# Products of 64 weight rows on the two row halves of the array, in a gated layer that goes by pairs of feature tiles

## The chip, the cores and the metric

The kernel runs on one core of a Trainium2 chip. The metric is the device time of one execution in microseconds (us). The kernel before takes 2023.67 us, the median of three runs that lie between 2023.3 and 2027.02.

## The reference

Four layers act in turn on x, 2048 tokens by 448 features: attention, gated layer, attention, gated layer. Both pairs use the same weights. Cut to what matters here:

```
def _B_ref(x, w_gate, w_up, w_down):      # x: 1 x 2048 x 448, F = 1792
    g = x @ w_gate                        # 448 x 1792
    u = x @ w_up                          # 448 x 1792
    return (sigmoid(g) * u) @ w_down      # 1792 x 448

x = x + _A_ref(layernorm(x), wqkv, wo)    # attention, 16 heads of 28
x = x + _B_ref(layernorm(x), w_gate, w_up, w_down)
x = x + _A_ref(layernorm(x), wqkv, wo)
x = x + _B_ref(layernorm(x), w_gate, w_up, w_down)
```

All inputs are float32.

## The kernel before

**Numbers in two halves.** TensorE multiplies 16-bit floats. A float32 operand is therefore split into a high float16 and a low float16 that holds the rest (`split`, line 170: the high part by ScalarE, the rest by VectorE). A product of two such operands is three products: high x high, high weights x low activations, low weights x high activations.

**The contraction of 448.** 448 rows are three tiles of 128 and a tail of 64. For the tail the high and the low part of the activations share one tile: `split_tail` (line 175) puts the high part on partitions 0 to 63 and the low part on 64 to 127. The weight tiles hold the last 64 rows twice, on both halves (`load_rows`, line 163). One product of the high weights with that tail tile thus gives two terms, and one of the low weights gives the last one (and the product of both low parts, which is too small to matter). So `by_features` (line 350) makes 3 x 3 + 2 = 11 matrix products of 128 x 128 weights with 512 tokens, all added up in one PSUM bank.

**The gated layer.** `gated` (line 977) goes over 4 blocks of 512 tokens and in each over 14 tiles of 128 hidden features. For a tile it makes the 11 products of the gate (bank 4), asks ScalarE for the sigmoid, makes the 11 products of up (bank 5), and asks VectorE for the product of both (line 1033) and `split` for its two halves `hhl`. The down products (`down`, line 991: 12 products of 448 columns, added up in banks 0 to 3 over all 14 tiles) run one tile later, behind the gate and up products of the next tile, so that the pointwise work has time. When a block's 14 tiles are added up, VectorE adds the result to x.

**The other work in the layer.** The next block of tokens is made ready along the way. `steps` (line 293) gives seven steps, taken one per feature tile from the third tile on by `run_fill`: `norm` (statistics on VectorE, the power on GpSimd), `squares` (scaling and 32 x 32 transposes on VectorE), `store` and `gather` (four DMAs to DRAM, two from the SyncE queue and two from ScalarE's, and two back, from SyncE), two empty steps, and two of `ready`, which split the 128-row tiles 0 and 1, then 2 and the tail. In the last block of the first layer `before_next` asks for the next layer's weights at feature tile 6. The first block of a layer is made ready in the output projection of the attention (`out_project`, line 922).

**What sets the order.** The program order is written by hand; nothing reorders it. Each engine takes its instructions in order and waits where a semaphore says so. SBUF is given out in slots from two lists, `big` (19 slots) and `qrt` (12), first freed first used. A name in the profile such as `sig_q` or `xhl_s` is the tile's name and its list.

**Array shapes.** The scores and the mix of attention (lines 821 and 839) use four strips of 32 columns of the array, by `tile_position`. The norm products of the projection (lines 485 and 488) have 16 weight columns and so use one strip. All others, apart from a few small ones at the start, use the full array.

Of the kernel before, what the change touches and what calls it, by code (L numbers as in the profile page):

```python
# [13 lines left out]
F16 = mybir.dt.float16  # L14
I32 = mybir.dt.int32
AF = mybir.ActivationFunctionType
ALU = mybir.AluOpType
AX = mybir.AxisListType

P = 128  # L20
# [6 lines left out]
NB = 4  # L27
TB = NT // NB
W = TB * P
NF = F // P  # L30
# [7 lines left out]
PS = 2.0 ** -14  # L38
# [45 lines left out]
def interleaved_layers(ctx: ExitStack, tc: tile.TileContext, x_in, wqkv, wo, w_gate, w_up,  # L84
                       w_down, out):
    nc = tc.nc
# [6 lines left out]
    big = Slots(spool, "s", N_SLOTS)  # L93
    qrt = Slots(spool, "q", N_QUART)
# [4 lines left out]
    def new_banks():  # L99

        if banks["stack"] is not None:
            banks["stack"].close()
        uid[0] += 1
        banks["stack"] = ExitStack()
        banks["pool"] = banks["stack"].enter_context(
            tc.tile_pool(name=f"psum{uid[0]}", bufs=1, space=bass.MemoryType.PSUM,
                         reuse_waits="tile"))

    def psum(tag, name, shape):
        uid[0] += 1  # L110
        return banks["pool"].tile(shape, F32, name=f"{name}_{uid[0]}", tag=tag, bufs=1)
# [4 lines left out]
    def bank(i, name):  # L116
        return psum(f"bank{i}", name, [P, 512])


    x = cpool.tile([P, NT, D], F32, name="x")  # L120
# [11 lines left out]
    up = cpool.tile([P, 7], F32, name="up")  # L132
# [37 lines left out]
    def split(hi, lo, raw):  # L170

        nc.scalar.copy(hi, raw)  # L172
        nc.vector.tensor_tensor(lo, raw, hi, op=ALU.subtract)  # L173

    def split_tail(tail, raw):

        nc.scalar.copy(tail[0:64], raw[0:64])
        nc.vector.tensor_tensor(tail[64:128], raw[0:64], tail[0:64], op=ALU.subtract)  # L178
# [38 lines left out]
    class Block:  # L217


        def __init__(self, b):  # L220
            self.b = b

        def norm(self, js=range(TB)):
            b = self.b
# [17 lines left out]
                                    op0=ALU.subtract, op1=ALU.mult)  # L242

        def parts(self):
            self.all = big.get("xhl", [P, 7, W], F16)
            self.hi, self.lo = self.all[:, 0:3, :], self.all[:, 3:6, :]
            self.tail = self.all[:, 6, :]


        def squares(self, js=range(TB)):  # L250
# [30 lines left out]
        def part(self, kt):  # L281

            raw = self.raw[:, kt, :].rearrange("p (i t c) -> p t i c", i=4, t=TB)
            order = "p (t i c) -> p t i c"
            if kt < 3:
                hi = self.hi[:, kt, :].rearrange(order, t=TB, i=4)
                lo = self.lo[:, kt, :].rearrange(order, t=TB, i=4)
                split(hi, lo, raw)
            else:
                split_tail(self.tail.rearrange(order, t=TB, i=4), raw)  # L290
                big.put(self.raw)

        def steps(self):
# [56 lines left out]
    def by_features(pm, blk, wh, wl, first_tile=None):  # L350

        order = [(wh, blk.hi), (wh, blk.lo), (wl, blk.hi)]
        terms = [(w(kt), x[:, kt, :]) for kt in range(3) for w, x in order]
        tails = [(w(3), blk.tail) for w in (wh, wl)]
        if first_tile == 0:
            terms = terms[0::3] + terms[2::3] + terms[1::3] + tails
        elif first_tile == 1:
            terms = terms[0::3] + terms[1::3] + tails[0:1] + terms[2::3] + tails[1:2]
        else:
            terms += tails  # L360
        for i, (w, x) in enumerate(terms):
            nc.tensor.matmul(pm, w, x, start=(i == 0), stop=(i == len(terms) - 1))  # L362

    def by_tokens(pm, hi, lo, tail, w, kts=range(4)):

# [93 lines left out]
    gate_scale = nc.scalar.alloc_register("gate_scale")  # L459

    def run_fill(fill, n=1):
        for _ in range(n):
            if fill:
                fill.popleft()()
# [457 lines left out]
    def out_project(outs, gate):  # L922
        new_banks()
        nc.scalar.activation(warm, warm, AF.Sigmoid)
        nc.scalar.reg_load(gate_scale, back.bitcast(I32)[0:1, 3:4])
        first = Block(0)
        steps = first.steps()
        steps = deque(steps[:5] + [lambda: None] * 4 + steps[5:])
        early = 6

        def products(pm, t, kts):
            by_tokens(pm, outs.hi(t), outs.lo(t), outs.tail(t) if 3 in kts else None, gate.out,
                      kts)

        def add(pm, t):
            nc.vector.scalar_tensor_tensor(x[:, t, :], pm, back[:, 1:2], x[:, t, :],  # L936
                                           op0=ALU.mult, op1=ALU.add)

        gate.load_dn()
        gate.load_gu()  # L940
        pms = [bank(t, "op")[:, 0:D] for t in range(early)]
        for t in range(early):
            products(pms[t], t, range(3))
        for t in range(early):
            products(pms[t], t, [3])
            add(pms[t], t)
            if t >= TB - 1:
                run_fill(steps)
        for t in range(early, NT):
            pm = bank(t % 6, "op")[:, 0:D]  # L950
            products(pm, t, range(4))
            add(pm, t)
            run_fill(steps)
        big.put(*outs.kt, gate.out)
        run_fill(steps, 9)
        return first
# [20 lines left out]
    def gated(layer, first, wt, before_next):  # L977
        last = layer == LAYERS - 1
        gu, dn = wt.gu, wt.dn
        while len(gu) < 7:  # L980
            wt.load_gu()
            if 2 * len(dn) < len(gu):
                wt.load_dn()

        seq = [(b, f) for b in range(NB) for f in range(NF)]
        blks = [first]
        steps = deque()
        pend = None
        accs = {}

        def down(b, f, hl):
            if f == 0:
                accs[b] = [bank(j, "dnp")[:, 0:D] for j in range(TB)]
            dw = dn[f // 4][:, f % 4]
            for j in range(TB):
                s = slice(j * P, (j + 1) * P)
                pm = accs[b][j]
                nc.tensor.matmul(pm, hl[:, 0, s], dw[:, 0, :], start=(f == 0), stop=False)  # L998
                nc.tensor.matmul(pm, hl[:, 0, s], dw[:, 1, :], start=False, stop=False)  # L999
                nc.tensor.matmul(pm, hl[:, 1, s], dw[:, 0, :], start=False, stop=(f == NF - 1))  # L1000
                if f == NF - 1:
                    t = b * TB + j
                    nc.vector.scalar_tensor_tensor(x[:, t, :], pm, back[:, 2:3], x[:, t, :],
                                                   op0=ALU.mult, op1=ALU.add)
                    if last:
                        nc.sync.dma_start(x_dst[:, t, :], x[:, t, :])
            qrt.put(hl)
            if b == NB - 1 and (f % 4 == 3 or f == NF - 1):
                big.put(dn[f // 4])

        for n, (b, f) in enumerate(seq):
            if f == 0:
                if b + 1 < NB:
                    blks.append(Block(b + 1))
                    steps.extend(blks[b + 1].steps())
                elif not last:
                    blks.append(Block(0))
                    steps.extend(blks[NB].steps())
            blk = blks[b]
            pgu = [bank(4, "gate"), bank(5, "up")]  # L1020
            c = slice((f % 2) * P, (f % 2 + 1) * P)
            g = gu[f // 2]
            for w in range(2):
                by_features(pgu[w], blk, lambda kt: g[:, w, 0, kt, c],
                            lambda kt: g[:, w, 1, kt, c])
                if w == 0:
                    sig = qrt.get("sig", [P, W])
                    nc.scalar.activation(sig, pgu[0], AF.Sigmoid, scale=gate_scale)  # L1028
            if b == NB - 1 and f % 2 == 1:
                big.put(g)  # L1030
            if f == NF - 1:
                blk.drop()
            nc.vector.scalar_tensor_tensor(sig, pgu[1], PS, sig, op0=ALU.mult, op1=ALU.mult)  # L1033
            hl = qrt.get("hhl", [P, 2, W], F16)
            split(hl[:, 0, :], hl[:, 1, :], sig)
            qrt.put(sig)
            if pend:
                down(*pend)
            pend = (b, f, hl)
            if 2 <= f:  # L1040
                run_fill(steps)
            if b == NB - 1 and not last:
                before_next(f)
        down(*pend)
        return blks[NB] if not last else None


# [3 lines left out]
    first = Block(0)  # L1051
# [28 lines left out]
    for layer in range(LAYERS):  # L1080
        values, heads, last_values = project(layer, wq, first)
        gate = WeightsGated()
# [4 lines left out]
        def before_next(f, wq=wq):  # L1087
            if f == 6:
                wq.load()

        first = gated(layer, mlp_first, gate, before_next)
# [28 lines left out]
```

## Time and profile before

| | |
|---|---|
| median of three runs | 2023.67 us |
| profiled execution | 2026.13 us |
| its span, first to last instruction | 2024.2 us |
| granted TensorE clock, mean | 0.998 |
| PE busy | 2005.5 us, 99% |
| weight loads (PEld) | 1028.8 us, 51% |
| VectorE (DVE) | 748.8 us, 37% |
| ScalarE (ACT) | 1189.6 us, 59% |
| GpSimd (POOL) | 33.3 us, 2% |

The first gate product starts at 625.7 us in the first layer and at 1625.7 in the second.

In a row of the groups stand the line, the engine, the operation, output<-inputs with their shapes and the count; then the busy time in us and the mean of one in ns; then the idle time of the engine just ahead, and what ended it. In a row of the order of time stand the start and the length in us, engine, line and operation, with the number of merged instructions (x11); products overlap, so the step from one start to the next is shorter than the length. In a row of the waits stand who waited for whom, the total in us, how many times, and the longest. In the table of stretches each engine has its busy time and, in brackets, its instructions, in the order PE, PEld, DVE, ACT, POOL, then clock, DMA share and GB/s.

### The profile page before, as it was taken

The page shows a single profiled execution, that of the slowest core. Times are in us where ns is not written, and L with a number is a line of the kernel's source. Part 1 is how long each engine was busy: PE and PEld are TensorE (multiplying, and loading weights), DVE is VectorE, ACT ScalarE, POOL GpSimd, SP SyncE. Part 2 cuts the span into 40 slices and gives each one's busy share as a digit, 9 for nine tenths or more (in the row PEclk, how much of TensorE's full clock was granted, in tenths as well). Part 3 has the DMA queues.
Part 4 walks back from the last instruction along what each step waited for, and adds up shares of the span by engine and source line. Part 5 has one row for each costly group of instructions (what it writes and reads, how often), then busy time and mean ns, then how long its engine had stood idle before and what let it go on. Part 6 is the DMA issues. An engine that isn't in the chain of part 4 may idle for free. (4 is left out here: it accounts for less than half of the span.)

```text
span 2024.2 us, 47829 instructions
## 1 busy us (share of the span) xinstructions
PE 2005.5 (99%) x21637; PEld 1028.8 (51%) x21637; DVE 748.8 (37%) x1110; ACT 1189.6 (59%) x1136; POOL 33.3 (2%) x75
## 2 busy tenths in 40 slices
PE   8999999999999999999999999999999999999999
PEld 4445555555554444444444555555555544444444
DVE  6635455551235232323274133222322432323222
ACT  5469999999961212121244799999999412121211
POOL 2000000000000000000000000000000000000000
PEclk9999999999999999999999999999999999999999
DMA  4563454741215100001143221121202250101000
GB/s 164 156 195 96 130 157 147 227 131 30 57 59 188 37 13 25 19 19 33 59 130 120 66 66 34 42 46 30 66 12 63 68 204 1 55 1 55 1 19 19
DMA packets 98630, 153.75 MB, mean 76 GB/s; under 512 B 9584, under 2 KB 79216, under 8 KB 95600
## 3 DMA queue, kind: packets, MB, share of 16 engines
q1 hardware_dynamic: 89728, 146.21, 23.9%
q10 hardware_dynamic: 8688, 4.36, 0.8%
q8 instruction: 174, 2.85, 0.6%
q14 instruction: 40, 0.33, 0.1%
HBM read 97.52 MB, written 45.68 MB: 71 GB/s over the span
## 5 line engine op out<-in xcount | busy, mean ns | idle before, releaser
L828 ACT ACTIVATE prob_s<-sc 128x1536 f32<-128x1536 f32 (+1 forms) x684 | 918.2, 1509 | 2.6 <-PE sc L821 1.4
L839 PE MATMUL acc<-prob_s,val_s 128*32 128x256 f32 x8192 | 571.7, 379 | 0.0
L821 PE MATMUL sc<-qp_s 114*32 114x512 f16 x8192 | 569.8, 380 | 1.5 <-ACT val_s L537 1.3
L362 PEld LDWEIGHTS <-gu_s 128*128 128x128 f16 x2464 | 241.1, 98 | 290.4 <-issue 6.4
L839 PEld LDWEIGHTS acc<-prob_s,val_s 128*32 128x32 f32 x8192 | 273.6, 110 | 179.8 <-ACT prob_s L828 0.4
L821 PEld LDWEIGHTS <-qp_s 114*32 114x32 f16 x8192 | 245.8, 95 | 222.3 <-issue 75.8
L362 PE MATMUL gate<-xhl_s,gu_s 128*128 128x512 f16 x1232 | 285.1, 379 | 4.2 <-ACT xhl_s L172 2.6
L362 PE MATMUL up<-xhl_s,gu_s 128*128 128x512 f16 x1232 | 284.2, 379 | 0.0
L1028 ACT ACTIVATE sig_q<-gate 128x512 f32<-128x512 f32 x112 | 66.9, 597 | 341.0 <-PE gate L362 324.8
L1033 DVE SCALAR_TENSOR_TENSOR sig_q<-up,sig_q 128x512 f32<-128x512 f32 x112 | 77.5, 692 | 460.9 <-PE up L362 460.9
L172 ACT CAST hhl_q<-sig_q 128x512 f16<-128x512 f32 x112 | 69.3, 618 | 288.1 <-DVE sig_q L1033 288.1
L853 DVE COPY oraw_q<-acc 128x512 f32<-128x512 f32 x32 | 22.1, 692 | 484.5 <-PE acc L839 484.4
L999 PE MATMUL dnp<-dn_s,hhl_q 128*128 128x448 f16 x448 | 157.9, 352 | 0.0
L998 PE MATMUL dnp<-dn_s,hhl_q 128*128 128x448 f16 x448 | 157.9, 352 | 0.0
L1000 PE MATMUL dnp<-dn_s,hhl_q 128*128 128x448 f16 x448 | 157.9, 352 | 0.0
L362 PE MATMUL qkp<-xhl_s,wqk_s 128*128 128x512 f16 x616 | 140.8, 380 | 0.9 <-DVE xhl_s L178 0.7
L855 DVE RECIPROCAL oden_q<-oden_q 128x512 f32<-128x512 f32 x32 | 107.3, 3353 | 1.1
L173 DVE TENSOR_TENSOR hhl_q<-sig_q,hhl_q 128x512 f16<-128x512 f32 x112 | 77.5, 692 | 76.7 <-ACT hhl_q L172 76.7
L362 PEld LDWEIGHTS <-wqk_s 128*128 128x128 f16 x616 | 57.2, 98 | 71.7 <-issue 4.5
L506 ACT ACTIVATE qkhl_q<-qkp 128x512 f16<-128x512 f32 x56 | 33.4, 596 | 65.5 <-PE qkp L362 65.4
L999 PEld LDWEIGHTS <-hhl_q 128*128 128x128 f16 x448 | 43.8, 98 | 43.8
L998 PEld LDWEIGHTS <-hhl_q 128*128 128x128 f16 x448 | 43.8, 98 | 43.8
(113 smaller groups left out, 1034.8 us busy)
## 6 DMA issues: line engine op xcount, KB each, us to landing
qp_s<-qk_scr SPq DMA_DIRECT2D x96, 224.0 KB
qk_scr<-qkhl_q SPq DMA_DIRECT2D x56, 256.0 KB
gu_s<-gu_parts SPq DMA_DIRECT2D x14, 1024.0 KB
xraw_s<-xt_scr SPq DMA_DIRECT2D x14, 768.0 KB
xt_scr<-xs_s SPq DMA_DIRECT2D x38, 224.0 KB
qp_s<-qk_scr SPq DMA_DIRECT2D x64, 112.0 KB
gu_parts<-pack_s SPq DMA_DIRECT2D x7, 1024.0 KB
raw_s<-in_B_w_down_dram SPq DMA_DIRECT2D x6, 896.0 KB
```

The lines of the kernel that those rows point to most:

```text
L172: nc.scalar.copy(hi, raw)
L173: nc.vector.tensor_tensor(lo, raw, hi, op=ALU.subtract)
L362: nc.tensor.matmul(pm, w, x, start=(i == 0), stop=(i == len(terms) - 1))
L821: nc.tensor.matmul(ps[32 * j:32 * j + 32, a, :], hd.k[:, keys], hd.q[:, qb * W:(qb + 1) * W], start=True, stop=True, tile_position=(0, 32 ...
L828: nc.scalar.activation(prob[:, 0:n, :], ps[:, 0:n, :], AF.Exp, scale=exp_scale)
L839: nc.tensor.matmul(acc[qb * VC:(qb + 1) * VC, n], v[:, kc % TB, h, :], probs[c * NB + qb][:, n], start=(kc == 0 and i % 2 == 0), stop=(kc ...
L855: nc.vector.reciprocal(den, den)
L998: nc.tensor.matmul(pm, hl[:, 0, s], dw[:, 0, :], start=(f == 0), stop=False)
L999: nc.tensor.matmul(pm, hl[:, 0, s], dw[:, 1, :], start=False, stop=False)
L1000: nc.tensor.matmul(pm, hl[:, 1, s], dw[:, 0, :], start=False, stop=(f == NF - 1))
L1028: nc.scalar.activation(sig, pgu[0], AF.Sigmoid, scale=gate_scale)
L1033: nc.vector.scalar_tensor_tensor(sig, pgu[1], PS, sig, op0=ALU.mult, op1=ALU.mult)
```

## The change

The gated layer goes over pairs of feature tiles. Four accumulators (gate and up of both tiles, banks 4 to 7) are filled one after the other with ten products each, all but the product of the low weights' last 64 rows. Those four come last, as products of 64 rows: the first and third on array rows 0 to 63, the second and fourth on rows 64 to 127. For this the high part of the activations' tail has to lie on partitions 64 to 127 too; a copy by ScalarE puts it into an eighth column of the block's tile (`upper`). Then come both sigmoids, both multiplications and both splits, and behind them the down products of the two tiles of the pair before. The steps for the next block are taken two at a time at the end of a pair. The product of both low parts of the tail is no longer made.

```diff
-        def __init__(self, b):
+        def __init__(self, b, twice=False):
             self.b = b
+            self.twice = twice
...
-            self.all = big.get("xhl", [P, 7, W], F16)
+            self.all = big.get("xhl", [P, 8, W], F16)
...
             self.tail = self.all[:, 6, :]
+            self.upper = self.all[:, 7, :]
...
                 split_tail(self.tail.rearrange(order, t=TB, i=4), raw)
+                if self.twice:
+                    nc.scalar.copy(self.upper[64:128].rearrange(order, t=TB, i=4), raw[0:64])
...
+    def by_features_in_fours(pms, blk, wh, wl):
+        for o, pm in enumerate(pms):
+            for kt in range(3):
+                nc.tensor.matmul(pm, wh(o, kt), blk.hi[:, kt, :], start=(kt == 0), stop=False)
+                nc.tensor.matmul(pm, wh(o, kt), blk.lo[:, kt, :], start=False, stop=False)
+                nc.tensor.matmul(pm, wl(o, kt), blk.hi[:, kt, :], start=False, stop=False)
+            nc.tensor.matmul(pm, wh(o, 3), blk.tail, start=False, stop=False)
+        for o, pm in enumerate(pms):
+            r = slice(64 * (o % 2), 64 * (o % 2) + 64)
+            x = blk.upper if o % 2 else blk.tail
+            nc.tensor.matmul(pm, wl(o, 3)[r], x[r], start=False, stop=True,
+                             tile_position=(r.start, 0))
...
-        first = Block(0)
+        first = Block(0, True)
...
-        seq = [(b, f) for b in range(NB) for f in range(NF)]
+        seq = [(b, p) for b in range(NB) for p in range(NF // 2)]
...
-            pgu = [bank(4, "gate"), bank(5, "up")]
-            c = slice((f % 2) * P, (f % 2 + 1) * P)
-            g = gu[f // 2]
-            for w in range(2):
-                by_features(pgu[w], blk, lambda kt: g[:, w, 0, kt, c],
-                            lambda kt: g[:, w, 1, kt, c])
-                if w == 0:
-                    sig = qrt.get("sig", [P, W])
-                    nc.scalar.activation(sig, pgu[0], AF.Sigmoid, scale=gate_scale)
+            g = gu[p]
+            pms = [bank(4 + i, "gate" if i % 2 == 0 else "up") for i in range(4)]
+
+            def part(i):
+                return lambda o, kt: g[:, o % 2, i, kt, (o // 2) * P:(o // 2 + 1) * P]
+
+            by_features_in_fours(pms, blk, part(0), part(1))
...
-            nc.vector.scalar_tensor_tensor(sig, pgu[1], PS, sig, op0=ALU.mult, op1=ALU.mult)
-            hl = qrt.get("hhl", [P, 2, W], F16)
-            split(hl[:, 0, :], hl[:, 1, :], sig)
-            qrt.put(sig)
-            if pend:
-                down(*pend)
-            pend = (b, f, hl)
-            if 2 <= f:
-                run_fill(steps)
-            if b == NB - 1 and not last:
-                before_next(f)
-        down(*pend)
+            sigs = [qrt.get("sig", [P, W]) for _ in range(2)]
+            hls = [qrt.get("hhl", [P, 2, W], F16) for _ in range(2)]
+            for a in range(2):
+                nc.scalar.activation(sigs[a], pms[2 * a], AF.Sigmoid, scale=gate_scale)
+                nc.vector.scalar_tensor_tensor(sigs[a], pms[2 * a + 1], PS, sigs[a],
+                                               op0=ALU.mult, op1=ALU.mult)
+            for a in range(2):
+                split(hls[a][:, 0, :], hls[a][:, 1, :], sigs[a])
+                qrt.put(sigs[a])
+            for d in pend:
+                down(*d)
+            pend = [(b, 2 * p + a, hls[a]) for a in range(2)]
+            for f in (2 * p, 2 * p + 1):
+                if 2 <= f:
+                    run_fill(steps)
+                if b == NB - 1 and not last:
+                    before_next(f)
+        for d in pend:
+            down(*d)
```

More of the change, by code (lines that the diff above doesn't have):

```diff
@@ L983, in gated @@
                 wt.load_dn()
-        seq = [(b, f) for b in range(NB) for f in range(NF)]
+        seq = [(b, p) for b in range(NB) for p in range(NF // 2)]
         blks = [first]
         steps = deque()
-        pend = None
+        pend = []
         accs = {}
@@ L1009, in down @@
                 big.put(dn[f // 4])
-        for n, (b, f) in enumerate(seq):
-            if f == 0:
+        for b, p in seq:
+            if p == 0:
                 if b + 1 < NB:
-                    blks.append(Block(b + 1))
+                    blks.append(Block(b + 1, True))
                     steps.extend(blks[b + 1].steps())
@@ L1019, in gated @@
             blk = blks[b]
-            pgu = [bank(4, "gate"), bank(5, "up")]
-            c = slice((f % 2) * P, (f % 2 + 1) * P)
-            g = gu[f // 2]
-            for w in range(2):
-                by_features(pgu[w], blk, lambda kt: g[:, w, 0, kt, c],
-                            lambda kt: g[:, w, 1, kt, c])
-                if w == 0:
-                    sig = qrt.get("sig", [P, W])
-                    nc.scalar.activation(sig, pgu[0], AF.Sigmoid, scale=gate_scale)
-            if b == NB - 1 and f % 2 == 1:
+            g = gu[p]
[3 more added lines that the diff above has]
+            by_features_in_fours(pms, blk, part(0), part(1))
+            if b == NB - 1:
                 big.put(g)
-            if f == NF - 1:
+            if p == NF // 2 - 1:
                 blk.drop()
-            nc.vector.scalar_tensor_tensor(sig, pgu[1], PS, sig, op0=ALU.mult, op1=ALU.mult)
-            hl = qrt.get("hhl", [P, 2, W], F16)
-            split(hl[:, 0, :], hl[:, 1, :], sig)
-            qrt.put(sig)
-            if pend:
-                down(*pend)
-            pend = (b, f, hl)
-            if 2 <= f:
-                run_fill(steps)
-            if b == NB - 1 and not last:
-                before_next(f)
-        down(*pend)
+            sigs = [qrt.get("sig", [P, W]) for _ in range(2)]
[17 more added lines that the diff above has]
+            down(*d)
         return blks[NB] if not last else None
```

## The prediction

> **What bounds the kernel now.** I read the page from the top, then the table of stretches, the chain of waits, the waits of TensorE, and last the order of time around the places that the change touches.
>
> ```profile
> span 2024.2 us, 47829 instructions
> PE 2005.5 (99%) x21637; PEld 1028.8 (51%) x21637; DVE 748.8 (37%) x1110; ACT 1189.6 (59%) x1136; POOL 33.3 (2%) x75
> ...
> PEclk9999999999999999999999999999999999999999
> ```
> ```profile
> 640.00:1040.00 400.00, 400.00 (x1936) 188.69 (x1935) 138.40 (x243) 82.56 (x138) 9.23 (x20) 1.00 0.11 34
> ```
> ```profile
> PE gate L362 <- ACT xhl_s L172: 2.6, 2, 1.5
> ```
>
> PE is busy in all of 640 to 1040 us, most of which is a gated layer, at full granted clock, with DVE at 138 and ACT at 83 of 400 us. The waits of PE that name this layer are those of its first products. So the layer is a queue of matrix products: its time is their number times their pitch (start to start). A busy PE is not a PE at its peak, so the pitch has to be read from starts:
>
> ```profile
> 645.75 2.54 PE L362 MATMUL gate<-xhl_s,gu_s 128*128 128x512 f16 x11
> 648.12 2.54 PE L362 MATMUL up<-xhl_s,gu_s 128*128 128x512 f16 x11
> 650.50 0.35 PE L998 MATMUL dnp<-dn_s,hhl_q 128*128 128x448 f16 x1
> ...
> 652.77 2.54 PE L362 MATMUL gate<-xhl_s,gu_s 128*128 128x512 f16 x11
> ```
>
> Eleven products take 648.12 - 645.75 = 2.37 us, so 0.216 us each; the twelve down products take 652.77 - 650.50 = 2.27, so 0.189 each. One feature tile is 7.02 us, a pair 14.04. There are 2 layers x 4 blocks x 14 tiles = 112 tiles, 56 pairs, so about 786 us of the run hangs on these pitches.
>
> **The change, part by part.** *The products taken together.* Each of the four accumulators of a pair ends with one product of the low weights' last 64 rows; these are 4 x 0.216 = 0.864 us per pair. Now they use 64 rows of the array each, lower and upper half in turn, in different PSUM banks. If two halves run side by side, two pitches remain: 0.432 us. The trace has no two row halves side by side. It has the nearest thing, four column strips side by side in attention:
>
> ```profile
> 170.47 0.84 PE L821 MATMUL sc<-qp_s 114*32 114x512 f16 x12
> 171.12 0.62 PE L839 MATMUL acc<-prob_s,val_s 128*32 128x256 f32 x8
> ```
>
> Twelve products of 512 columns start within 0.65 us: 0.054 each, or 0.216 for four, exactly the pitch of one full product. The overlap of strips is complete there, with a weight load for each. Ends for a pair of row halves: 0.216 us (complete) and 0.432 (none). I take 0.216, as the strips row does, since row halves are addressed in the same way and read different partitions.
>
> *The change of array shape.* A pair now leaves the full array once and comes back once. The norm products (128 rows by 16 columns) do just that between full products:
>
> ```profile
> 1085.09 2.55 PE L362 MATMUL qkp<-xhl_s,wqk_s 128*128 128x512 f16 x11
> 1087.57 0.28 PE L485 MATMUL qnorm<-sq_q,ind 128*16 128x256 bf16 x1
> 1087.77 2.55 PE L362 MATMUL qkp<-xhl_s,wqk_s 128*128 128x512 f16 x11
> 1090.25 0.28 PE L485 MATMUL qnorm<-sq_q,ind 128*16 128x256 bf16 x1
> 1090.37 0.27 PE L488 MATMUL knorm<-sq_q,ind 128*16 128x256 bf16 x1
> 1090.57 1.69 PE L362 MATMUL qkp<-xhl_s,wqk_s 128*128 128x512 f16 x7
> ```
> ```profile
> 1087.56 0.09 PEld L485 LDWEIGHTS <-ind 128*16 128x16 bf16 x1 [0.42 <-issue]
> ```
>
> From one group of eleven to the next are 1087.77 - 1085.09 = 2.68 us. Eleven full pitches are 2.37, and 256 columns are half a pitch, 0.108. The excursion, in and out, costs 2.68 - 2.37 - 0.108 = 0.20 us. The weight-load row shows why: the load stands idle until its product begins, where it is otherwise done a product ahead. For the first step inside the new shape and the offset of the second half behind the first I add 0.02: qnorm to knorm is 0.12 us where half a pitch is 0.108, and I estimate 0.01 for the offset. Ends for the excursion: 0.20, and 0.40 if each of the two weight loads at entry and at exit is exposed by its duration as well (the page has 98 ns for one):
>
> ```profile
> L362 PEld LDWEIGHTS <-gu_s 128*128 128x128 f16 x2464 | 241.1, 98 | 290.4 <-issue 6.4
> ```
>
> I take 0.20, since the measured excursion already has an exposed load at each end.
>
> [...]
>
> Per pair: 0.864 - (0.432 + 0.20 + 0.02) = 0.212 us saved; 56 pairs: 11.9 us. A pair then lasts 14.04 - 0.21 = 13.83 us.
>
> *The order by pairs.* Gate and up of both tiles, 44 products, come before the pointwise work, and two tiles of down products (24 x 0.189 = 4.54 us) follow. Before, the sigmoid ran beside the up products; now sigmoids and multiplications begin only at the end of the four. What covers them is the down work of the pair before.
>
> ```profile
> 641.11 2.54 PE L362 MATMUL up<-xhl_s,gu_s 128*128 128x512 f16 x11
> ```
> ```profile
> 643.75 0.69 DVE L1033 SCALAR_TENSOR_TENSOR sig_q<-up,sig_q 128x512 f32<-128x512 f32 x1 [4.96 <-PE up L362]
> 645.13 0.69 DVE L173 TENSOR_TENSOR hhl_q<-sig_q,hhl_q 128x512 f16<-128x512 f32 x1 [0.68 <-ACT hhl_q L172]
> 645.74 0.62 DVE L231 BATCH_NORM_STATS2 st<-x 128x6 f32<-128x448 f32 x1
> ...
> 648.57 0.18 DVE L232 BATCH_NORM_AGGREGATE mv<-st 128x2 f32<-128x6 f32 x1
> ...
> 652.75 0.51 DVE L240 TENSOR_SCALAR xn_s<-x,mv,rs 128x448 f32<-128x448 f32 x1
> ...
> 656.52 0.65 DVE L257 STREAM_TRANSPOSE xs_s<-xn_s 128x448 f32<-128x448 f32 x1
> ```
> ```profile
> L1028 ACT ACTIVATE sig_q<-gate 128x512 f32<-128x512 f32 x112 | 66.9, 597 | 341.0 <-PE gate L362 324.8
> ...
> L172 ACT CAST hhl_q<-sig_q 128x512 f16<-128x512 f32 x112 | 69.3, 618 | 288.1 <-DVE sig_q L1033 288.1
> ```
>
> The last up product starts at 641.11 + 10 x 0.216 = 643.27 and DVE follows at 643.75: 0.48 later. Call S the start of the first half-array product. Sigmoids run from S+0.48 to S+1.7, multiplications to S+2.5, casts to S+3.2, subtractions to S+3.9. PE returns from the excursion at S+0.55 and finishes the down work at S+5.1. The next pair's first gate product needs the first sigmoid (S+1.1), its first up product, at S+7.2, the first multiplication (S+1.8): covered by 4.0 and 5.4 us. Where that cover is gone it costs: the first pair of each layer has no down work behind it. PE, free at S+0.55, waits until about S+1.12: 0.57 us, twice, 1.1 us in all.
>
> *The steps for the next block* (norm, transposes, store and gather, split) now come two at a time. In the second pair DVE goes on from S+3.9: norm 648.75 - 645.74 = 3.0 us, POOL's two instructions, transposes 657.17 - 652.75 = 4.4:
>
> ```profile
> 1607.04 0.20 POOL L235 TENSOR_SCALAR rs<-mv 128x4 f32<-128x4 f32 x1 [487.07 <-DVE mv L232]
> ...
> 1607.32 1.02 POOL L237 TENSOR_TENSOR rs<-rs,nhalf 128x4 f32<-128x4 f32 x1
> ```
>
> That ends near S+12.8, before the next multiplication (13.83 + 1.12 = S+14.95): free, with 2.1 us to spare, and PE would feel it only 5.4 us after that. The store's half on SP goes when the transposes end, its half on ACT behind the third pair's casts, at S+17. Store and gather take 6.20 and 5.38 us where the chain of waits shows them:
>
> ```profile
> 1613.24 6.20 DMA xt_scr<-xs_s
> 1619.63 5.38 DMA xraw_s<-xt_scr
> ```
>
> With about 1.5 us of issuing they land near S+30. The first split stands on ACT behind the fourth pair's casts, at 27.66 + 3.2 = S+30.9. If it waits there, the next sigmoid stands behind it, due at S+42.0; that leaves some 10 us. The weights for the next layer (three loads on SP) are asked for half a pair later, more than 40 us before their use. The added ACT copy of 64 rows, about 0.61 us as the casts are, comes once per block, 8 times, on an engine that has 80% free here; the first block's copy ends before that layer's first sigmoid. All of this I cost at nothing.
>
> *Sum.* 0.212 x 56 = 11.87 us saved, 1.14 us lost: -10.7 us. The profiled execution took 2026.13 us, of which its span is 2024.2; it would take 2015.4. It lies 2.46 us above the median of the runs, 2023.67, from which I subtract: 2013.0 us, 0.53% less. What this measurement can tell from no change is about 0.2%, 4 us.
>
> **The rivals.** *The halves overlap in part.* For it: a half's weights have all 128 columns, where a strip's have 32, and a load takes 98 ns. Against it: full products with such loads keep the pitch of 0.216. If half a load is exposed for each pair of halves, these take 0.27 us: 0.104 saved per pair of tiles, 5.8 - 1.1 = 4.7 us, so 2019.0. Saving ends where two halves take 0.31 us.
> [...]
>
> *The halves run one after the other* (slower). For it: nothing in the trace shows two row groups at once. Then the four products still take 0.864 us and the excursion comes on top: 0.22 x 56 = 12.3, with the first pairs 13.4: 2037.1 us. It decides from the 0.31 us above. That the change would not do what it says is this case.
>
> *The pointwise work becomes the bound.* The multiplications would have to come 5.4 us late at a pair; the second pair has DVE work to S+12.8 and is the only candidate. Were it 10 us late, 4.6 us of stall in each of 7 blocks would cost 32 us: 2045. The sums above speak against it.
>
> **How the numbers follow.** Complete overlap 0.72 (2013.0; its own range, with an excursion of 0.17 to 0.24 us, 2011 to 2016), partial 0.12 (2016 to 2024), none 0.11, the pointwise bound or an unforeseen wait 0.05. The range 2010.5 to 2021 holds the first and most of the second, near 0.8. Faster by over 0.2% (below 2019.6): 0.72 + 0.08 = 0.80; within 0.2%: 0.04 of the partial case and 0.01 of the last, 0.05; slower: 0.15.
>
> **What would show it.** In the profile after: two half-row products that start within some 20 ns of each other, the next two 0.22 us later, about 0.3 us from a full product's start to the first half and from the last half to the next down product; pairs 13.8 us apart; one wait of PE for the sigmoid of 0.6 us per layer. Starts 0.216 apart inside the four would make the prediction wrong, as would a wait of PE for a sigmoid or multiplication in any pair but the first.

## The result, and the profile after

The changed kernel takes 2015.8 us (median of four runs, 2013.17 to 2017.36); the kernel before, run beside it, 2025.26 (2023.3 to 2027.02). The ratio is 0.9954, with an interval of 0.9939 to 0.9968: faster by 0.46%, or 9.5 us between the medians. The profiled executions differ by 10.5 us (spans of 2024.2 and 2013.7).

The page of the changed kernel, its first lines, and the waits of TensorE (who waited for whom, total, times, longest):

```profile
span 2013.7 us, 47841 instructions
...
PE 1994.9 (99%) x21637; PEld 1007.1 (50%) x21637; DVE 739.1 (37%) x1110; ACT 1187.7 (59%) x1144; POOL 33.3 (2%) x75
```
```profile
PE gate L373 <- ACT xhl_s L172: 3.3, 2, 2.3
...
PE gate L373 <- ACT sig_q L1053: 0.9, 2, 0.5
```

PE has the same number of products and is as full as before, only for 10.6 us less. One new wait has come, for the sigmoid, twice, once in each layer. The busy share stays 99% although the kernel gets faster: TensorE is the bound before and after, and since products overlap (a full one is 0.38 us long, and the next starts 0.216 us after it), two at once fill its row no more than one. So the gain has to be read from the starts of the products.

The order of time on TensorE around one group of half-array products (start, length, line, output), and the start of the next group, one pair of tiles later:

```profile
684.86 0.38 PE L376 MATMUL up<-xhl_s,gu_s 128*128 128x512 f16 x1
685.18 0.39 PE L380 MATMUL gate<-xhl_s,gu_s 64*128 64x512 f16 x1
685.18 0.39 PE L380 MATMUL up<-xhl_s,gu_s 64*128 64x512 f16 x1
685.40 0.38 PE L380 MATMUL gate<-xhl_s,gu_s 64*128 64x512 f16 x1
685.40 0.38 PE L380 MATMUL up<-xhl_s,gu_s 64*128 64x512 f16 x1
685.71 0.36 PE L1017 MATMUL dnp<-dn_s,hhl_q 128*128 128x448 f16 x1
685.91 0.35 PE L1018 MATMUL dnp<-dn_s,hhl_q 128*128 128x448 f16 x1
...
698.99 0.39 PE L380 MATMUL gate<-xhl_s,gu_s 64*128 64x512 f16 x1
```

Two halves start together, the next two 0.22 us later. The way into the half array takes 685.18 - 684.86 = 0.32 us where a pitch (start to start) of full products is 0.216, the way out 685.71 - 685.40 = 0.31. From group to group are 698.99 - 685.18 = 13.81 us, where two feature tiles took 14.04. All 50 steps from one pair to the next, from the third pair of each layer on, are 13.82 us long. The rows say f16: the products of the gated layer are of 16-bit floats. That is not so of the whole kernel, as the description above may sound; the mix of attention has rows with f32 inputs (128x256 f32).

Where the profiled difference lies is read from stage to stage, from the first product of one to that of the next, and in the last layer to the end of its last product. The first gated layer takes 394.3 us before and 388.7 after, the second 394.5 and 389.7: 5.6 and 4.7 us less, 10.4 together with the rounding. The starting stretch and the other stages lie between 2.5 us less and 0.9 us more, and come to 0.1 in sum.

### The profile page after: what moved, and what is told of

Its sections match the earlier page's. It is cut to its first block, busy times and chain, and to the rows that moved or that the text cites. A ratio compares the mean times of both kernels' runs of the same rounds, so it can differ in the third digit from the quotient of the medians.

```text
span 2013.7 us, 47841 instructions
## 1 busy us (share of the span) xinstructions
PE 1994.9 (99%) x21637; PEld 1007.1 (50%) x21637; DVE 739.1 (37%) x1110; ACT 1187.7 (59%) x1144; POOL 33.3 (2%) x75
## 5 line engine op out<-in xcount | busy, mean ns | idle before, releaser
L1053 ACT ACTIVATE sig_q<-gate 128x512 f32<-128x512 f32 x112 | 60.8, 595 | 598.2 <-PE up L380 598.2
L1054 DVE SCALAR_TENSOR_TENSOR sig_q<-up,sig_q 128x512 f32<-128x512 f32 x112 | 72.3, 686 | 514.7 <-ACT sig_q L1053 514.6
L373 PE MATMUL gate<-xhl_s,gu_s 128*128 128x512 f16 x336 | 127.7, 380 | 4.2 <-ACT xhl_s L172 3.3
L374 PE MATMUL gate<-xhl_s,gu_s 128*128 128x512 f16 x336 | 127.8, 380 | 1.0 <-DVE xhl_s L173 1.0
L375 PE MATMUL gate<-xhl_s,gu_s 128*128 128x512 f16 x336 | 127.8, 380 | 0.0
L373 PE MATMUL up<-xhl_s,gu_s 128*128 128x512 f16 x336 | 127.6, 380 | 0.0
L374 PE MATMUL up<-xhl_s,gu_s 128*128 128x512 f16 x336 | 127.5, 379 | 0.0
L375 PE MATMUL up<-xhl_s,gu_s 128*128 128x512 f16 x336 | 127.3, 379 | 0.0
L374 PEld LDWEIGHTS <-gu_s 128*128 128x128 f16 x672 | 65.8, 98 | 82.4 <-issue 5.2
L375 PEld LDWEIGHTS <-gu_s 128*128 128x128 f16 x672 | 65.9, 98 | 81.2 <-issue 2.6
L373 PEld LDWEIGHTS <-gu_s 128*128 128x128 f16 x672 | 65.8, 98 | 79.1 <-issue 2.0
```

Source lines behind the costliest of these rows:

```text
L373: nc.tensor.matmul(pm, wh(o, kt), blk.hi[:, kt, :], start=(kt == 0), stop=False)
L374: nc.tensor.matmul(pm, wh(o, kt), blk.lo[:, kt, :], start=False, stop=False)
L375: nc.tensor.matmul(pm, wl(o, kt), blk.hi[:, kt, :], start=False, stop=False)
L1054: nc.vector.scalar_tensor_tensor(sigs[a], pms[2 * a + 1], PS, sigs[a], op0=ALU.mult, op1=ALU.mult)
```

## The experiments

The theory: two row halves overlap completely, an excursion to the half array and back costs 0.2 us once per group, and the pointwise work stays hidden. Rivals: the order by pairs brings the gain; 64-row products are short by themselves; the excursion is hidden anyway.

**Full products in the new order.**

```diff
-            r = slice(64 * (o % 2), 64 * (o % 2) + 64)
-            x = blk.upper if o % 2 else blk.tail
-            nc.tensor.matmul(pm, wl(o, 3)[r], x[r], start=False, stop=True,
-                             tile_position=(r.start, 0))
+            nc.tensor.matmul(pm, wl(o, 3), blk.tail, start=False, stop=True)
```

> The order by pairs is kept, but the four last products of a pair are full ones again (128 rows, the low weights with the whole tail tile). Theory (the gain is the overlap of the row halves): a pair lasts 14.04 us as in the kernel before, no product has 64 rows, the first pair of each layer waits 0.26 us for its sigmoid (first tail product to sigmoid end 1.12, less 4 x 0.216), so the time is that of the kernel before plus 0.5 us. Rival (the order by pairs itself brings the gain): a pair lasts 13.82 us and the time is some 10 us below the kernel before.

Measured: 2025.08 us against 2026.63, ratio 0.9994 (0.9984 to 1.0003). The ratios here are those on record; for this kernel and the next three they differ a little from the quotients of the medians shown, which are 0.9992, 1.0053, 0.9995 and 0.9936. The order of time, with the four last products and the first one's successor a pair later:

```profile
685.65 0.38 PE L378 MATMUL gate<-xhl_s,gu_s 128*128 128x512 f16 x1
685.86 0.38 PE L378 MATMUL up<-xhl_s,gu_s 128*128 128x512 f16 x1
686.08 0.38 PE L378 MATMUL gate<-xhl_s,gu_s 128*128 128x512 f16 x1
686.30 0.38 PE L378 MATMUL up<-xhl_s,gu_s 128*128 128x512 f16 x1
699.68 0.38 PE L378 MATMUL gate<-xhl_s,gu_s 128*128 128x512 f16 x1
```

From pair to pair are 699.68 - 685.65 = 14.03 us, the 14.04 of the kernel before but for rounding: the order alone brings nothing, and costs nothing that the times can show. In the order of time the first pair of each layer waits 0.20 us for its sigmoid, where 0.26 was expected. The gain is in how the last four products are made.

**All four on one half.**

```diff
-            r = slice(64 * (o % 2), 64 * (o % 2) + 64)
-            x = blk.upper if o % 2 else blk.tail
+            r = slice(0, 64)
+            x = blk.tail
```

> All four 64-row products of a pair use the lower half of the array. Theory: nothing overlaps, so they take four pitches of 0.216 and the excursion of 0.21 comes on top: a pair lasts 14.25 us, and the time is 12 us above the kernel before. Rival (products of 64 rows are shorter by themselves): a pair stays at 13.82 us and the time at that of the changed kernel.

Measured: 2037.41 us against 2026.63, ratio 1.0059 (1.0042 to 1.0075): 10.8 us more by the medians, 12 by the ratio. The order of time:

```profile
685.71 0.38 PE L376 MATMUL up<-xhl_s,gu_s 128*128 128x512 f16 x1
686.02 0.39 PE L380 MATMUL gate<-xhl_s,gu_s 64*128 64x512 f16 x1
686.25 0.38 PE L380 MATMUL up<-xhl_s,gu_s 64*128 64x512 f16 x1
686.46 0.38 PE L380 MATMUL gate<-xhl_s,gu_s 64*128 64x512 f16 x1
686.68 0.38 PE L380 MATMUL up<-xhl_s,gu_s 64*128 64x512 f16 x1
686.99 0.36 PE L1017 MATMUL dnp<-dn_s,hhl_q 128*128 128x448 f16 x1
...
700.27 0.39 PE L380 MATMUL gate<-xhl_s,gu_s 64*128 64x512 f16 x1
```

A product of 64 rows takes a full pitch, and a pair lasts 700.27 - 686.02 = 14.25 us, 0.21 above the 14.04 of before. That is 11.8 us for 56 pairs. It shows the excursion alone, and the slower rival as it would have looked; the rival that products of 64 rows are short by themselves is ruled out. Against 13.82 it gives the overlap its size: 0.43 us per pair, two pitches.

**An excursion for each feature tile.**

```diff
             nc.tensor.matmul(pm, wh(o, 3), blk.tail, start=False, stop=False)
-        for o, pm in enumerate(pms):
-            r = slice(64 * (o % 2), 64 * (o % 2) + 64)
-            x = blk.upper if o % 2 else blk.tail
-            nc.tensor.matmul(pm, wl(o, 3)[r], x[r], start=False, stop=True,
-                             tile_position=(r.start, 0))
+            for h in (o - 1, o) if o % 2 else ():
+                r = slice(64 * (h % 2), 64 * (h % 2) + 64)
+                x = blk.upper if h % 2 else blk.tail
+                nc.tensor.matmul(pms[h], wl(h, 3)[r], x[r], start=False, stop=True,
+                                 tile_position=(r.start, 0))
```

> The two 64-row products of each feature tile follow that tile's full products, so a pair makes two excursions of two products and not one of four. Theory (each excursion costs its own 0.20 us): two products in halves cost 0.216 + 0.20 = 0.42 us where two full ones cost 0.432, so nearly all of the gain is gone: a pair lasts 14.01 to 14.04 us, the time is 0 to 2 us below the kernel before. Rival (most of the excursion hides beside other work, and the gain is simply the number of halves): a pair lasts 13.8 us, the time is that of the changed kernel.

Measured: 2025.65 us against 2026.63, ratio 0.9998 (0.9988 to 1.0007). From a pair's second group to that of the next:

```profile
680.69 0.39 PE L380 MATMUL gate<-xhl_s,gu_s 64*128 64x512 f16 x1
680.70 0.39 PE L380 MATMUL up<-xhl_s,gu_s 64*128 64x512 f16 x1
681.02 0.39 PE L373 MATMUL gate<-xhl_s,gu_s 128*128 128x512 f16 x1
...
694.72 0.39 PE L380 MATMUL gate<-xhl_s,gu_s 64*128 64x512 f16 x1
```

14.03 us: the halves overlap as before, but two excursions eat it all. Pairing the feature tiles is therefore what makes the half-array products pay: it lets four of them share one excursion.

**A spare bank for the first accumulator.**

```diff
-            pms = [bank(4 + i, "gate" if i % 2 == 0 else "up") for i in range(4)]
+            pms = [bank(0 if i + b + p == 0 else 4 + i, "gate" if i % 2 == 0 else "up")
+                   for i in range(4)]
```

> The first gate accumulator of a layer takes bank 0, which the down products need only a pair later, so that the second pair's first bank is free at once. Theory: the one wait for the sigmoid of each layer (0.53 us) goes, 1.1 us less than the changed kernel, too little for the times but plain in the waits of PE; bank 0 was last read by the addition of token tile 12, which stands ahead of the first block's splits, so nothing new is waited for. Rival (the second gate or the first up product waits in its place): the wait moves and the first two pairs of a layer keep their length of 24.9 us.

Measured: 2013.74 us against 2026.63, ratio 0.9943 (0.9926 to 0.9959). The wait for the sigmoid is gone from TensorE's list, and nothing stands in its place. The first gate product of the layer and that of the third pair, first here, then in the changed kernel:

```profile
623.29 0.38 PE L373 MATMUL gate<-xhl_s,gu_s 128*128 128x512 f16 x1 [0.79 <-ACT xhl_s L172]
...
647.67 0.38 PE L373 MATMUL gate<-xhl_s,gu_s 128*128 128x512 f16 x1
```
```profile
623.90 0.38 PE L373 MATMUL gate<-xhl_s,gu_s 128*128 128x512 f16 x1 [0.94 <-ACT xhl_s L172]
...
648.81 0.38 PE L373 MATMUL gate<-xhl_s,gu_s 128*128 128x512 f16 x1
```

24.38 us against 24.91: 0.53 us in the first layer, where the list of waits has 0.5 for the longest. (The second layer's first two pairs take 24.39 us against 25.80; there a stretch at half clock, of which more below, is gone as well.) The two intervals overlap, so the times alone do not separate this version from the changed kernel; the profile does.

**Lower, lower, upper, upper.**

```diff
-        for o, pm in enumerate(pms):
+        for o, pm in [(i, pms[i]) for i in (0, 2, 1, 3)]:
             r = slice(64 * (o % 2), 64 * (o % 2) + 64)
```

> The four 64-row products of a pair go lower, lower, upper, upper and no longer in turn. Theory (products start in program order, and two overlap only as neighbours on different halves): the second lower product waits a pitch for the first, the first upper one starts beside it, the second upper one a pitch later: three pitches in place of two, a pair lasts 13.82 + 0.22 = 14.04 us, and the time is that of the kernel before plus 1 us (the first pairs' waits). Rival (the engine takes an upper product ahead of a waiting lower one): a pair stays at 13.82 us and the time at that of the changed kernel.

Measured: 2015.33 us against 2024.86, ratio 0.9952 (0.9936 to 0.9968). The theory was wrong here. The kernel's text gives gate, gate (lower half), up, up (upper half); the order of time gives

```profile
684.33 0.39 PE L380 MATMUL gate<-xhl_s,gu_s 64*128 64x512 f16 x1
684.34 0.39 PE L380 MATMUL up<-xhl_s,gu_s 64*128 64x512 f16 x1
684.56 0.38 PE L380 MATMUL gate<-xhl_s,gu_s 64*128 64x512 f16 x1
684.56 0.38 PE L380 MATMUL up<-xhl_s,gu_s 64*128 64x512 f16 x1
...
698.15 0.39 PE L380 MATMUL gate<-xhl_s,gu_s 64*128 64x512 f16 x1
```

An up product starts 0.01 us after the first gate product, 0.22 us ahead of the second, which stands before it in the program. The pair keeps 13.82 us. So the products of the two halves need not alternate in this program; TensorE started the up product of the upper half ahead of the second gate product of the lower one. The statement above that each engine takes its instructions in order therefore does not hold for these products on TensorE.

**Pointwise work made late.** Idle multiplications on VectorE between the first sigmoid and the first multiplication of each pair, five of them in one kernel and nine in another (the lines are those of the first):

```diff
+            late = qrt.get("late", [P, W])
             for a in range(2):
                 nc.scalar.activation(sigs[a], pms[2 * a], AF.Sigmoid, scale=gate_scale)
+                for _ in range(5 if a == 0 else 0):
+                    nc.vector.scalar_tensor_tensor(late, pms[1], PS, sigs[0], op0=ALU.mult,
+                                                   op1=ALU.mult)
...
+            qrt.put(late)
```

> Five idle multiplications of 0.69 us stand on DVE between the first sigmoid and the first multiplication of every pair, 3.45 us in all. Theory (the down products of the pair before cover the pointwise work by 5.4 us at the first up product): the first multiplication ends at S+5.3 where it is due at S+7.2, also behind the second pair's norm and transposes (S+6.6), so all pairs but the first keep 13.82 us. Rival (the cover is shorter, DVE near to the bound): pairs get longer, by up to 3.45 us each.

> The same with nine idle multiplications, 6.2 us. Theory: the first multiplication ends at S+8.0, 0.8 us past its due time, so a pair lasts 14.6 us; behind the second pair of a block DVE starts 3.3 us late on top, and the span comes to some 2085 to 2100 us. Rival (something else covers more, or the waits meet before the up product): pairs of 13.82 us, or of well over 15 us.

Measured, one run of each and so without an interval: 2021.98 us with five, 2131.17 with nine. With five, every pair from the third on keeps 13.82 us; the some 6 us come from the first two pairs of each layer, 27.1 and 28.8 us long, and from the last down products of each, which wait for their operand. The second pair waits 2.03 us in both layers; the rows of the order of time, and those of the table of stretches behind them (TensorE's clock is the third number from the end), are

```profile
638.68 0.38 PE L373 MATMUL up<-xhl_s,gu_s 128*128 128x512 f16 x1 [2.03 <-DVE sig_q L1058]
1637.54 0.47 PE L373 MATMUL up<-xhl_s,gu_s 128*128 128x512 f16 x1 [2.03 <-DVE sig_q L1058]
```
```profile
638.70:642.20 3.50, 3.50 (x17) 1.61 (x17) 1.82 (x3) 1.18 (x2) 0.00 (x0) 1.00 0.37 143
1637.70:1641.20 3.50, 3.50 (x10) 1.25 (x9) 1.67 (x3) 1.03 (x2) 0.00 (x0) 0.51 0.36 144
```

In the second layer 3.4 us at half clock follow, in the first none; the second layer's two pairs are 1.7 us longer, half of that. The waits of TensorE with nine, and the order of time at one of its pairs:

```profile
PE up L373 <- DVE sig_q L1058: 78.2, 54, 4.9
```
```profile
707.82 0.38 PE L373 MATMUL up<-xhl_s,gu_s 128*128 128x512 f16 x1 [0.91 <-DVE sig_q L1058]
...
714.39 0.39 PE L380 MATMUL gate<-xhl_s,gu_s 64*128 64x512 f16 x1
...
729.28 0.39 PE L380 MATMUL gate<-xhl_s,gu_s 64*128 64x512 f16 x1
```

The wait stands where the theory put it, at the first up product, and in all 54 pairs that follow another of their layer. Its sizes were too low: a pair lasts 729.28 - 714.39 = 14.89 us and not 14.6, the pair behind a norm and transposes 19.6, and the span, 2129.1 us, is 29 us above the 2085 to 2100 given. Nine idle multiplications took 6.5 us where 6.2 were reckoned, which accounts for the 0.3 us per pair. A pair 1.07 us longer for work 6.5 us later gives a cover of 5.4 us, as reckoned. Much of the rest of the excess lies in the seven pairs behind norm and transposes. In the later ones the wait is 3.92 us in place of 0.91, 3.0 us more, as against 3.3 expected; behind each of these waits the clock was half for 3.4 us (the granted clock is 0.50 from 785.30 to 788.70), which makes the other 1.7 of the 4.7 us. The expectation had no term for that.

**Products that fill the wait at the layer's start**, on top of the spare bank:

```diff
+        pm = bank(7, "still")[:, 0:D]
+        for i in range(6):
+            nc.tensor.matmul(pm, gate.out[:, 0, 0, 0:P], gate.out[:, 0, 1, :], start=(i == 0),
+                             stop=(i == 5))
         big.put(*outs.kt, gate.out)
         run_fill(steps, 9)
```

> The spare bank for the first gate accumulator, and six products of 448 columns with a result that nobody reads at the end of the output projection, where PE waits for the first block's splits. Theory (a wait of PE of 2 us and more at that place is followed by 3.4 us at half clock, one of 1.5 us is not): the wait is 1.1 us shorter, no stretch of half clock is left at the second gated layer, its first two pairs take 24.4 us in every profile, and the time is that of the spare bank alone or up to 0.9 us less. Rival (the half clock there comes by itself, whatever PE does): it shows up with the short wait too.

Measured: 2013.28 us against 2024.86, ratio 0.9943 (0.9926 to 0.9959). What led to it is in the changed kernel's order of time at the second gated layer, and in its table of stretches:

```profile
1619.93 0.38 PE L373 MATMUL gate<-xhl_s,gu_s 128*128 128x512 f16 x1 [2.33 <-ACT xhl_s L172]
...
1621.81 0.63 PE L375 MATMUL gate<-xhl_s,gu_s 128*128 128x512 f16 x1
1622.24 0.63 PE L373 MATMUL gate<-xhl_s,gu_s 128*128 128x512 f16 x1
```
```profile
1621.00:1625.00 4.00, 4.00 (x13) 1.48 (x11) 3.36 (x6) 1.05 (x2) 0.00 (x0) 0.57 1.01 416
```

After a wait of 2.33 us the pitch is 1622.24 - 1621.81 = 0.43 us, twice the normal one, for most of 4 us, and the granted clock is 0.57. The second layer's first two pairs take 25.80 us there against 24.91 in the first. With the six products in place the same stretch reads

```profile
1621.00:1625.00 4.00, 3.75 (x17) 1.65 (x17) 2.03 (x4) 0.00 (x0) 0.00 (x0) 1.00 1.01 418
```

and both layers' first two pairs take 24.38 us. Over the profiles, a half clock followed this wait where it was 2.0 us or more (2.0, 2.3, 2.4, 2.5, 2.5) and did not where it was at most 1.8 (1.4, 1.4, 1.5, 1.8); the kernel before, with 1.5, lies on the good side. The length alone does not settle it: with five idle multiplications a wait of 2.03 us, at the second pair, was followed by half clock in one layer and not in the other. The length of this wait varies from run to run, so one profile with the filled wait does not prove that the wait is the cause. The spare bank alone had a wait of 1.4 us and no half clock either; the times of the two are not apart.

## Why the prediction was right, point by point

**The bound.** Right: the layer is a queue of products, and the order by pairs with full products (14.03 us per pair, no change of time) shows that the order by itself does not move it.

**The products taken together.** Right: 0.22 us for two halves, as the column strips had shown. The partial and the missing overlap are ruled out by the order of time; the kernel with all on one half shows what the missing one costs, 10.8 to 12 us, where 13.4 had been reckoned for it. The 13.4 counted the 1.1 us of the first pairs in full, though four products one after the other leave less of the sigmoid to wait for: in that kernel the first pair waits about 0.1 us. That 0.216 us would hold for row halves was carried over from column strips, as the prediction said; nothing in the trace before had shown it.

**The excursion.** Right: 0.20 + 0.02 us taken; the one-half kernel gives 0.21 above four full pitches, the order of time about 0.10 each way. Of the 0.02 us, 0.01 for the offset of the second half was the author's estimate, read off no row; after the change the two halves start 0.00 to 0.01 us apart. The price read from products of 128 rows by 16 columns (0.20 us) held for 64 rows by 128.

**The order by pairs.** Right: one wait for the sigmoid per layer, 0.53 us by the spare bank, where 0.57 was reckoned. The cover of the later pairs came out of the kernel with nine idle multiplications as reckoned, 5.4 us.

**The steps for the next block.** Right as far as TensorE shows it: in the changed kernel it waits for no multiplication and for no sigmoid but those of each layer's first pair.

**The sum.** -10.7 us were forecast. The pairs gave 0.22 rather than 0.212 each, 56 x 0.22 = 12.3, less 1.1 for the first pairs: -11.2. The profile has -10.4 in the two layers, since the half clock at the second layer's start, which the sum did not contain, took 0.9 of it. So the pairs saved 0.5 us more than reckoned in sum and the half clock took 0.9 back; that the total lies so near is in part luck. The medians differ by 9.5, inside an interval that reaches from 6.5 to 12.4. The time itself came out as 2015.8 us where 2013.0 was forecast: 1.6 of the 2.8 us is that the kernel before measured 2025.26 beside it and not 2023.67, and the other 1.2 is the 9.5 us that were saved where 10.7 were forecast.

## What to carry to other kernels

Work with half a contraction was free only in company: two row halves overlapped completely here (0.22 us for both, and 0.22 us for each on one half), but each excursion to the half array and back cost about 0.2 us, nearly one product of 512 columns (0.216 us). Two such products per excursion gained nothing and four gained 0.22 us, so collect at least four. The cost of an excursion could be read before the change off a narrow product that stands between full ones, as the distance between the starts of the full ones less the pitches. When an order is changed so that results come in larger lots, look first at the start of each stage, where no earlier lot covers them; a bank that is still idle there can take the first one.

## What the runs showed of the hardware that was not expected

TensorE started products of different row halves out of program order. In the kernel with lower, lower, upper, upper the first upper product started 0.01 us after the first lower one and 0.22 us before the second. The pair's length of 13.82 us, in place of the 14.04 expected with products in order, agrees with the starts. How far ahead a product can start was not tried.

A single wait of TensorE of some 2 us in a stretch that is otherwise full was in most cases followed by 3.4 us at half clock, which cost 0.9 us in the changed kernel's profile. Six of the seven waits of 2.0 to 2.5 us in the gated layers were followed by it, none of 1.8 us or less, and all eleven of 3.8 us or more, in the kernel with nine idle multiplications, came with one; what decides for those of 2 us stays open. In the changed kernel the stretch came 1.3 us after the end of a wait of 2.33 us, from 1621.2 to 1624.6 us. Such stretches may be a part of the scatter of the times: of the 27 executions of the kernel before that ran beside the experiments, the 14 of at most 2026.17 us had a mean granted clock of 0.998 or 0.999, and 12 of the 13 longer ones had 0.997.
